# Half-size reloads of the second weight in a 20-product MLP behind sigmoid attention: single blocks kept in float32 and split on arrival, a new product order, a last store in three

## Chip, core and metric

The kernel runs on one core of one Trainium2 chip. The metric is the device time of one execution in microseconds. The engines are called as the profile calls them: PE (TensorE, matmul; PEld is its weight load), ACT (ScalarE), DVE (VectorE), POOL (GpSimd) and SP (SyncE, which here issues every DMA).

## What is computed

Eight batches of twelve heads, 448 tokens, head width 64. Attention uses a sigmoid instead of a softmax; its result, 3584 tokens by 768, goes through an MLP of width 2048.

```python
scores = scale * np.matmul(q, k.transpose(0, 1, 3, 2)) - np.log(S)
attn = 1.0 / (1.0 + np.exp(-scores))
attn_out = np.matmul(attn, v)
x = attn_out.transpose(0, 2, 1, 3).reshape(B * S, H * D)
h = x @ w_in
g = h * (1.0 / (1.0 + np.exp(-1.702 * h)))
return g @ w_out
```

All arrays are float32. The weights reach the kernel as raw words of a 64-bit type and are turned into float32 on the chip.

## The kernel before

**Precision.** Every float32 operand of a large product is held as two float32r parts: a rounded part `hi` and the rest `lo = value - hi`. A product of two such operands is three matmuls (lo by hi, hi by lo, hi by hi; `TERMS`, line 41). To "split" is to make the two parts: one copy that rounds (ACT or DVE, lines 759 and 760 for weights, 1001 and 1002 for activations) and one subtraction on DVE (lines 762 and 1013).

**Three stages.** Attention comes first; while it runs on PE, DVE and ACT decode the sixteen weight tiles (`decode`, line 456) and DMAs store twelve of them as float32 in DRAM (`whole`, names `f` in the trace). The tokens make seven blocks of 512. The first block is multiplied in the ordinary way (`first_block`, line 808): `up(n)` is a part of the first product (matmuls `h<-x,w`), `down(n)` a part of the second (matmuls `o_q<-g,w`), each `down` 36 matmuls long, in the order up 0, up 1, down 0, up 2, down 1, ..., up 7, down 6, down 7. Blocks 1 to 3 and 4 to 6 are two groups (`triple`, line 947). In a group each of the two weight products is replaced by 20 products of sums of blocks instead of 24 products of blocks (tables at lines 44 to 48): `W_SUMS`, `X_SUMS` and `G_SUMS` say which sums of weight and activation blocks enter product r, `H_SUMS` and `O_SUMS` how the 20 results are added. Each product is 36 matmuls of 128x512 (name `p`). `m` is 0 for the first weight and 1 for the second, `h` (0 or 1) is a half of a weight block.

**Weights in DRAM.** While the first block runs, the split parts of all twenty weight operands of both weights are saved in DRAM (`save`, line 772; DRAM names `c`), to be loaded by both groups. An operand is either a single block (six of the twenty: `W_USES[r] < 8`) or a sum of blocks. Single blocks are split for the first block's own use in `pieces` (line 814) and saved from there, two parts at once, 768 KB for each half: 12 saves for each weight (`c<-w` of 768 KB). Sums are made by `sums_ahead` (line 905) and saved (`c<-wc`); the right half of `h = 1` is made inside the first group from quarter loads (`wq<-f`).

**Weights in a group.** `pieces_of(m, r)` (line 965) takes a buffer from a ring of four (`wsplit`) for each half `h`, and loads the two parts from `c` (`w<-c`). A product uses two buffers, so the buffers of product k come free when product k-2 is done with them.

**Order of the work.** `SEQUENCES` (line 49) gives the order of the 40 products (m, r) of each group. It sets which x blocks (`x<-xd`, 768 KB each) are needed when, and how the results are added: `Net` decides by the distance between products whether a result goes on in PSUM (a chain), is put back there by ACT (a seed, line 1102), is copied out (line 1141) or is added by DVE out of PSUM (line 1175). Two PSUM tiles of four banks alternate.

**The planner.** The program's order on ACT, DVE and SP is made by `Plan.run` (line 104): a list scheduler with assumed costs. A task's `key` is the place of its first user in PE's order; an engine takes the ready task of least key. A task that needs a slot of SBUF may take one when its key is at most `HORIZON` = 14 tasks ahead. A DMA is assumed to end after all planned DMAs before it (2.7 ns for each KB) plus a landing time. The chip then runs each queue in that fixed order. `store` (line 1189) copies an output from PSUM where needed and issues its store; the last output of the second group is copied by ACT with a factor of -1 (line 1197), 1536 columns at once, then stored as 768 KB.

Of the kernel before, what the change touches and what calls it, by code (L numbers as in the profile page):

```python
# [8 lines left out]
F32 = mybir.dt.float32  # L9
# [23 lines left out]
HORIZON, URGENT, SPARE, KEEP = 14, 4, 1, 2  # L33
AWAY = 3

ATTENTION, LATE = ("qk", "vraw", "a", "al", "raw64", "e", "qkraw", "x32"), ("wsplit",)
# [11 lines left out]
O_SUMS = ([(20, [(9, 1), (17, -1)]), (21, [(5, 1), (10, 1)]), (22, [(4, 1), (12, 1)]), (23, [(21, 1), (22, -1)]), (24, [(18, 1), (23, 1)]), (25, [(1, 1), (11, 1)]), (26, [(0, 1), (20, 1)]), (27, [(25, 1), (26, 1)]), (28, [(8, 1), (15, 1)]), (29, [(3, 1), (13, 1)])], [[(4, -1), (6, -1), (20, 1), (28, 1)], [(9, 1), (19, 1), (24, 1)], [(1, -1), (7, 1), (24, 1), (29, 1)], [(12, -1), (16, 1), (27, -1), (28, -1)], [(5, -1), (14, -1), (27, -1)], [(0, -1), (2, 1), (21, -1), (29, -1)]])  # L48
SEQUENCES = ([(0, 16), (0, 18), (0, 19), (0, 12), (0, 3), (0, 10), (0, 8), (0, 14), (0, 11), (0, 2), (0, 5), (0, 15), (0, 17), (1, 3), (0, 1), (0, 4), (0, 7), (0, 13), (0, 6), (1, 8), (1, 4), (1, 18), (1, 12), (0, 9), (1, 5), (1, 16), (0, 0), (1, 19), (1, 2), (1, 13), (1, 15), (1, 9), (1, 10), (1, 14), (1, 7), (1, 1), (1, 0), (1, 6), (1, 17), (1, 11)], [(0, 18), (0, 19), (0, 14), (0, 10), (0, 3), (0, 12), (0, 13), (0, 2), (0, 1), (0, 5), (0, 11), (0, 17), (0, 7), (0, 9), (0, 15), (0, 0), (0, 6), (1, 2), (1, 9), (1, 0), (0, 16), (1, 3), (0, 4), (1, 5), (0, 8), (1, 10), (1, 16), (1, 4), (1, 15), (1, 8), (1, 13), (1, 19), (1, 17), (1, 12), (1, 1), (1, 6), (1, 18), (1, 14), (1, 11), (1, 7)])

# [27 lines left out]
class Plan:  # L78
# [25 lines left out]
    def run(self, streams):  # L104
# [43 lines left out]
        def since(t):  # L148
            when = t.ready
            for b in t.holds:  # L150
                if b.slot is None:
                    if not (t.anytime or t.key <= doing + HORIZON):
                        return math.inf
                    found = place(b, t)
                    if found is None:
                        return math.inf
                    when = max(when, found[0])
            return when
# [162 lines left out]
def sigmoid_attention_mlp(ctx: ExitStack, tc: tile.TileContext, qk, v, w, out):  # L321
# [486 lines left out]
    def first_block():  # L808
# [5 lines left out]
        def pieces(m, h, i, got):  # L814
            out = []
            for k in range(2):
                node = nodes[m, h, 2 * i + k] = got[k]
                b, into, first = (weights_slot if count[0] < 2 else weights_ring)(f"w{m}_{h}_{i}_{k}")
                t = split_piece(node, PIECE, into, b, first)
                if count[0] < 2:  # L820
                    for u in b.users:
                        u.anytime = True
                count[0] += 1
                for r in used_as(2 * i + k):
                    save(m, r, h, slice(0, PIECE), into, b, t)
                out.append((t, b, into))
            return out
# [119 lines left out]
    def triple(one, blocks_before):  # L947
# [17 lines left out]
        def pieces_of(m, r):  # L965
            out = []
            for h in range(2):
                b, into, first = weights_ring(f"w{m}_{one}_{r}_{h}")
                ts = []
                if W_USES[r] >= 8 and h and one == 1:  # L970
                    node = w_sums[m].get(W_USES[r])
# [52 lines left out]
        def products(m, r, sums, uses, n, parts, sign, onto, deps):  # L1024
            pieces = pieces_of(m, r)
            t_x, xb = pair_of(sums, uses[r][0], n, f"{'xg'[m]}p{one}_{uses[r][0]}", sign)
            ps, tag, more = onto
            edge = [*(blocks_before[tag] if len(plan.rings[tag]) == 1 else []), *deps]
            for i in range(parts):
# [14 lines left out]
                units_of.setdefault((m, r), []).append([t])  # L1044
            return t

        class Net:
# [34 lines left out]
            def product(self, r, onto):  # L1082
# [26 lines left out]
                t = products(self.m, r, sums, uses, (XB, GB)[self.m], self.parts, sign, (ps, tag, more), deps)  # L1109
                node = Node(ps, lambda: ps.tile[:, : self.parts].rearrange("p a b -> p (a b)"), [t])  # L1110
                if more:
# [76 lines left out]

        def store(i, sign, node, kind):
            if kind == "psum":  # L1190
                bank = node
                b, view = nets[1].slot(("out", i))
                if sign > 0:
                    t = on_either((act(XB), lambda: nc.scalar.copy(view(), bank.view())),
                                  (dve(XB), lambda: nc.vector.tensor_copy(view(), bank.view())), node.done, [b, node.b])
                else:
                    t = task("ACT", act(XB), lambda: nc.scalar.mul(view(), bank.view(), -1.0), node.done, [b, node.b])
                node.readers.append(t)
                node = Node(b, view, [t])
            else:  # L1200
                assert sign > 0
            k, n = divmod(i, 3)
            dma(lambda: out[one + n, k * NJ : (k + 1) * NJ].rearrange("j p t -> p j t"),
                lambda: node.view().rearrange("p (j t) -> p j t", j=NJ), P * XB * 4 / 1024, node.done, [node.b])

# [67 lines left out]
```

## Time and profile before

| | us |
|---|---|
| median of 3 runs | 1074.75 (1072.87 to 1075.59) |
| the profiled execution | 1073.19 |
| its span, first to last instruction | 1071.4 |
| PE busy in it | 1046.7 |
| DVE busy in it | 808.7 |
| ACT busy in it | 556.5 |
| mean granted TensorE clock (1 is 2.4 GHz) | 0.993 |

The span is what the trace covers; the profiled execution took 1.8 us more than that. PE is the bounding engine over most of the span, so idle time of the others matters only where PE waits for it. Attention takes about 0 to 263 us, the first block 263 to 402, the first group 408 to 735, the second 735 to 1065.

### The profile page before, as it was taken

The page shows a single profiled execution, that of the slowest core. Times are in us where ns is not written, and L with a number is a line of the kernel's source. Part 1 is how long each engine was busy: PE and PEld are TensorE (multiplying, and loading weights), DVE is VectorE, ACT ScalarE, POOL GpSimd, SP SyncE. Part 2 cuts the span into 40 slices and gives each one's busy share as a digit, 9 for nine tenths or more (in the row PEclk, how much of TensorE's full clock was granted, in tenths as well). Part 3 has the DMA queues.
Part 4 walks back from the last instruction along what each step waited for, and adds up shares of the span by engine and source line. Part 5 has one row for each costly group of instructions (what it writes and reads, how often), then busy time and mean ns, then how long its engine had stood idle before and what let it go on. Part 6 is the DMA issues. An engine that isn't in the chain of part 4 may idle for free.

```text
span 1071.4 us, 13585 instructions
## 1 busy us (share of the span) xinstructions
PE 1046.7 (98%) x5300; PEld 780.1 (73%) x5300; DVE 808.7 (75%) x733; ACT 556.5 (52%) x534; POOL 0.2 (0%) x4
## 2 busy tenths in 40 slices
PE   8999999999999987999999999999999999999997
PEld 5454545454788865888888888888888888888886
DVE  5988788873988755689789778997684676777683
ACT  7887888886555433545463344433444253433342
POOL 0000000000000000000000000000000000000000
PEclk9999999999999998999999999999999999999999
DMA  9899999883999999666677767699865656565665
GB/s 348 305 329 383 338 343 325 312 293 119 376 408 372 395 393 359 234 216 230 211 233 225 236 227 237 227 311 369 277 220 194 205 177 206 175 204 182 217 230 201
DMA packets 110799, 290.30 MB, mean 271 GB/s; under 512 B 8720, under 2 KB 69264, under 8 KB 108688
## 3 DMA queue, kind: packets, MB, share of 16 engines
q1 hardware_dynamic: 110736, 289.44, 76.6%
q8 instruction: 42, 0.69, 0.2%
q14 instruction: 21, 0.17, 0.0%
HBM read 195.04 MB, written 94.37 MB: 270 GB/s over the span
## 4 chain that ended last, share of the span: by engine, by line
PE 91%; DMA 6%; DVE 1%; ACT 1%; issue 1%; SPq 0%; DVEq 0%; ACTq 0%
PE p L796 60%; PE av L604 10%; PE sc L573 8%; PE h L796 5%; PE o_q L796 4%; DMA c<-wc 2%; PE av L617 2%; DMA x<-xd 1%; PE sc L589 1%; DMA xd<-x 1%; DMA wq<-f 1%; DMA qkraw<-qk 0%; DMA w<-c 0%; DVE qk L444 0%; ACT graw L852 0%
## 5 line engine op out<-in xcount | busy, mean ns | idle before, releaser
L796 PE MATMUL p<-xp,w 128*128 128x512 f32 x1440 | 330.5, 391 | 7.7 <-DVE xp L1013 5.9
L796 PE MATMUL p<-gp,w 128*128 128x512 f32 x1440 | 328.0, 389 | 0.1
L796 PEld LDWEIGHTS p<-xp,w 128*128 128x128 f32 x1440 | 271.6, 189 | 65.4 <-DVE xp L1013 6.3
L796 PEld LDWEIGHTS p<-gp,w 128*128 128x128 f32 x1440 | 270.2, 188 | 56.6 <-DMA w<-c 0.5
L559 ACT ACTIVATE a<-sc,bias 128x896 f32<-128x896 f32 x168 | 158.5, 1019 | 15.1 <-PE sc L573 10.9
L604 PE MATMUL av<-a,vraw 128*64 128x448 f32 x576 | 118.6, 547 | 0.1
L573 PEld LDWEIGHTS sc<-qk 64*128 64x128 f32 x846 | 75.8, 184 | 41.9 <-issue 13.8
L573 PE MATMUL sc<-qk 64*128 64x448 f32 x846 | 98.6, 373 | 3.4 <-DVE qk L444 2.3
L604 PEld LDWEIGHTS av<-a,vraw 128*64 128x64 f32 x576 | 37.1, 136 | 59.7 <-issue 56.1
L1141 ACT COPY o<-p 128x1536 f32<-128x1536 f32 x23 | 33.1, 1445 | 90.3 <-PE p L796 60.9
L1141 ACT COPY h<-p 128x2048 f32<-128x2048 f32 x19 | 35.6, 1874 | 78.1 <-PE p L796 59.6
L796 PE MATMUL o_q<-g,w 128*128 128x512 f32 x288 | 68.5, 396 | 5.2 <-ACT w L759 3.5
L1013 DVE TENSOR_TENSOR gp<-h,gp 128x2048 fp32r<-128x2048 f32 x29 | 66.4, 2289 | 5.7 <-ACT gp L1001 5.3
L1175 DVE TENSOR_TENSOR h<-h,p 128x2048 f32<-128x2048 f32 x20 | 45.3, 2286 | 31.9 <-ACT h L1141 17.8
L796 PEld LDWEIGHTS o_q<-g,w 128*128 128x128 f32 x288 | 54.9, 192 | 17.9 <-ACT w L759 3.9
L796 PE MATMUL h<-x,w 128*128 128x512 f32 x288 | 66.6, 390 | 1.3 <-DVE x L656 1.3
L796 PEld LDWEIGHTS h<-x,w 128*128 128x128 f32 x288 | 54.0, 188 | 13.3 <-DVE x L656 2.1
L444 DVE TENSOR_TENSOR qk<-qkraw,qk 128x896 fp32r<-128x896 f32 x47 | 51.2, 1089 | 6.1 <-ACT qk L438 5.6
L1001 ACT CAST gp<-h 128x2048 fp32r<-128x2048 f32 x19 | 36.3, 1913 | 36.9 <-PE p L796 28.6
L1175 DVE TENSOR_TENSOR o<-o,p 128x1536 f32<-128x1536 f32 x20 | 34.7, 1751 | 23.0 <-PE p L796 13.9
L739 DVE TENSOR_TENSOR h<-h,h 128x2048 f32<-128x2048 f32 x21 | 48.0, 2289 | 0.5 <-ACT h L1183 0.2
L656 DVE COPY x<-av 128x64 f32<-128x64 f32 (+6 forms) x42 | 16.9, 413 | 36.0 <-ACT x L654 31.2
(106 smaller groups left out, 963.2 us busy)
## 6 DMA issues: line engine op xcount, KB each, us to landing
w<-c SPq DMA_DIRECT2D x76, 768.0 KB, 5.2
w<-c SPq DMA_DIRECT2D x140, 384.0 KB, 4.4
w<-w SPq DMA_DIRECT2D x16, 1536.0 KB, 10.2
c<-wc SPq DMA_DIRECT2D x56, 384.0 KB, 7.4
qkraw<-qk SPq DMA_DIRECT2D x47, 448.0 KB, 6.4
c<-w SPq DMA_DIRECT2D x24, 768.0 KB, 7.6
vraw<-v SPq DMA_DIRECT2D x24, 448.0 KB, 4.9
xd<-x SPq DMA_DIRECT2D x42, 256.0 KB, 4.7
```

The source lines that it names most:

```text
L444: lambda: nc.vector.tensor_tensor(lo(), src(), hi().bitcast(F32), op=ALU.subtract),
L559: nc.scalar.activation(a.tile, ps.tile[:, :, :S], AF.Sigmoid, bias=bias, scale=scale)
L573: nc.tensor.matmul(ps.tile[:, j, :S], lhsT=src[kk][rows, S + c * P : S + (c + 1) * P], rhs=src[qq][rows, :S], start=i == 0, stop=i == len( ...
L604: nc.tensor.matmul(ps.tile[cols, n % 2, :S], lhsT=vr.tile[:, at : at + D], rhs=a.tile[:, j], start=c == 0, stop=False, skip_group_check=True,)
L617: nc.tensor.matmul(ps.tile[cols, k, :S], lhsT=vr.tile[rows, at : at + D], rhs=a.tile[rows, j], start=False, stop=True, skip_group_check=True,)
L656: (0.15 + 0.00105 * n, lambda xb=xb, into=into, cols=cols: nc.vector.tensor_copy(xb.tile[:, into], ps.tile[:, bank, cols])),
L739: return task("DVE", cost, lambda: nc.vector.tensor_tensor(out(), x(), y(), op=op), deps, uses)
L796: nc.tensor.matmul(ps, lhsT=ws[:, a, c * P : (c + 1) * P], rhs=x[:, d, k], start=start and i == 0 and j == 0, stop=stop and i == len(todo) ...
L1001: t_hi = on_either((act(n), lambda: nc.scalar.copy(part(0)(), node.view())), (cast(n), lambda: nc.vector.tensor_copy(part(0)(), node.view())),
L1013: nc.vector.tensor_tensor(part(1)(), node.view(), part(0)().bitcast(F32), op=ALU.subtract)
L1141: t = on_either((act(self.n), lambda: nc.scalar.copy(view(), node.view())), (dve(self.n), lambda: nc.vector.tensor_copy(view(), node.view())),
L1175: nc.vector.tensor_tensor(view(), x.view(), y.view(), op=ALU.add if s0 == s else ALU.subtract)
```

## The change

**Reloads.** For the second weight (`AGAIN`: m = 1, both halves) the saves of split single blocks in `pieces` are left out: 12 saves of 768 KB. In both groups `pieces_of` loads such a block (six products for each group, two halves each, 24 loads) in float32 from `whole`, 384 KB, into the second part of its ring buffer, and splits it there: the rounding copy on ACT or DVE, the subtraction on DVE.

**Planner.** A DMA whose key lies more than `PRESSING` = 4 tasks ahead isn't planned to start before the planned DMA backlog is down to `BACKLOG` = 6 us.

**Order.** The first group has a new sequence; that of the second stays.

**Last store.** Where the last output of the second group comes out of PSUM, its three 512-column parts are copied and stored one by one, each after the matmuls of that part. `products` therefore returns the task of each part.

```diff
+AGAIN = ((1, 0), (1, 1))
+BACKLOG, PRESSING = 6.0, 4
...
-SEQUENCES = ([(0, 16), (0, 18), (0, 19), (0, 12), (0, 3), (0, 10), (0, 8), (0, 14), (0, 11), (0, 2), (0, 5), (0, 15), (0, 17), (1, 3), (0, 1), (0, 4), (0, 7), (0, 13), (0, 6), (1, 8), (1, 4), (1, 18), (1, 12), (0, 9), (1, 5), (1, 16), (0, 0), (1, 19), (1, 2), (1, 13), (1, 15), (1, 9), (1, 10), (1, 14), (1, 7), (1, 1), (1, 0), (1, 6), (1, 17), (1, 11)], [...
+SEQUENCES = ([(0, 19), (0, 8), (0, 10), (0, 18), (0, 2), (0, 16), (0, 12), (0, 1), (0, 14), (0, 15), (0, 11), (0, 7), (0, 17), (0, 4), (0, 0), (0, 5), (1, 8), (0, 9), (0, 3), (1, 4), (1, 12), (0, 13), (1, 3), (1, 18), (0, 6), (1, 16), (1, 9), (1, 10), (1, 2), (1, 19), (1, 14), (1, 15), (1, 17), (1, 7), (1, 1), (1, 13), (1, 11), (1, 0), (1, 5), (1, 6)], [...
...
         def since(t):
             when = t.ready
+            if "SP" in t.costs and t.key > doing + PRESSING:
+                when = max(when, free["DMA"] - BACKLOG)
...
-                for r in used_as(2 * i + k):
+                for r in used_as(2 * i + k) if (m, h) not in AGAIN else ():
                     save(m, r, h, slice(0, PIECE), into, b, t)
...
                 b, into, first = weights_ring(f"w{m}_{one}_{r}_{h}")
                 ts = []
+                if W_USES[r] < 8 and (m, h) in AGAIN:
+                    i, k = divmod(W_USES[r], 2)
+                    n = (2 * m + h) * 4 + i
+                    at = k * NW_EL
+                    t = dma(lambda into=into: into()[:, 1].bitcast(F32), lambda n=n, at=at: whole[n][:, at : at + NW_EL],
+                            KB, [stored[n], *gate], [b], first)
+                    t = split_piece(Node(b, lambda into=into: into()[:, 1].bitcast(F32), [t]), PIECE, into, b)
+                    out.append(([t], b, into))
+                    continue
...
+                last = one + 3 == NB and all(left < 0 for left in nets[1].left.values())
+                parts = [slice(j, j + 1) for j in range(NJ)] if last else parts
...
+            for end, part in zip(ends, parts):
+                cols = slice(part.start * T, part.stop * T)
...
+                    else:
+                        end = task("ACT", act(n), lambda cols=cols, copied=copied: copied(nc.scalar.mul, cols, -1.0),
+                                   [end], [b, bank.b])
+                    bank.readers.append(end)
+                done.append(end)
+                dma(lambda part=part: into[:, part], lambda cols=cols: view()[:, cols].rearrange("p (j t) -> p j t", t=T),
+                    P * n * 4 / 1024, [end], [b])
```

## Rows read from the trace of the kernel before

**Rows 1.** The page: busy time of each engine; DMA busy in 40 slices.
```profile
PE 1046.7 (98%) x5300; PEld 780.1 (73%) x5300; DVE 808.7 (75%) x733; ACT 556.5 (52%) x534; POOL 0.2 (0%) x4
...
DMA  9899999883999999666677767699865656565665
```

**Rows 2.** Timeline of PE, 350 to 425 us: start, us, work, idle before and its releaser.
```profile
379.21 8.32 PE L796 MATMUL o_q<-g,w 128*128 128x512 f32 x36
391.06 0.49 PE L796 MATMUL o_q<-g,w 128*128 128x512 f32 x1 [3.53 <-ACT w L759]
392.05 9.62 PE L796 MATMUL o_q<-g,w 128*128 128x512 f32 x35 [0.50 <-DVE w L762]
407.56 10.60 PE L796 MATMUL p<-xp,w 128*128 128x512 f32 x36 [5.89 <-DVE xp L1013]
419.94 5.25 PE L796 MATMUL p<-xp,w 128*128 128x512 f32 x22 [1.78 <-issue]
```

**Rows 3.** Timeline of ACT from 1060 us to the end.
```profile
1065.53 1.45 ACT L1197 ACTIVATE o<-p 128x1536 f32<-128x1536 f32 x1 [13.39 <-PE p L796]
```

**Rows 4.** Windows of 20 us: each engine's busy time, then PEclk, DMA share, GB/s.
```profile
280.00:300.00 20.00, 18.89 (x83) 15.67 (x84) 19.90 (x31) 11.19 (x16) 0.00 (x0) 1.00 1.02 377
...
320.00:340.00 20.00, 20.00 (x90) 16.57 (x89) 17.04 (x29) 11.27 (x19) 0.00 (x0) 1.00 0.98 360
...
380.00:400.00 20.00, 15.98 (x64) 12.58 (x63) 10.89 (x19) 7.67 (x13) 0.00 (x0) 0.91 1.03 387
400.00:420.00 20.00, 12.33 (x45) 9.37 (x43) 6.82 (x7) 6.72 (x6) 0.00 (x0) 0.83 1.04 413
```

**Rows 5.** What PE waited for from 0 to 366 us: total, times, longest.
```profile
PE sc L573 <- DVE qk L444: 2.3, 2, 1.8
```

**Rows 6.** The chain that ended last, between 340 and 425 us: start, us, what.
```profile
379.68 6.78 DMA wq<-f
...
394.15 10.06 DMA x<-xd
404.24 1.48 ACT xp L1001
```

**Rows 7.** A window of 2.5 us, columns as in rows 4.
```profile
422.50:425.00 2.50, 2.50 (x12) 2.07 (x12) 2.50 (x3) 0.00 (x0) 0.00 (x0) 1.00 0.33 127
```

**Rows 8.** DMAs issued from 366 to 425 us; the last column is the median us to landing.
```profile
DMA packets 9080, 22.80 MB, mean 386 GB/s; under 512 B 684, under 2 KB 6253, under 8 KB 9077
...
x<-xd SPq DMA_DIRECT2D x4, 768.0 KB, 10.2
c<-w SPq DMA_DIRECT2D x3, 768.0 KB, 8.5
```

**Rows 9.** DMAs issued from 750 to 1060 us, columns as in rows 8.
```profile
w<-c SPq DMA_DIRECT2D x82, 384.0 KB, 4.3
w<-c SPq DMA_DIRECT2D x33, 768.0 KB, 4.4
```

**Rows 10.** Groups by line and shape: count | busy us, mean ns | idle before, releasers.
```profile
L1013 DVE TENSOR_TENSOR gp<-h,gp 128x2048 fp32r<-128x2048 f32 x29 | 66.4, 2289 | 5.7 <-ACT gp L1001 5.3
L1175 DVE TENSOR_TENSOR o<-o,p 128x1536 f32<-128x1536 f32 x20 | 34.7, 1751 | 23.0 <-PE p L796 13.9 <-ACT o L1141 9.0
L762 DVE TENSOR_TENSOR w<-wf,w 128x768 fp32r<-128x768 f32 x16 | 15.0, 956 | 5.0 <-ACT w L759 4.9
L759 ACT CAST w<-wf 128x768 fp32r<-128x768 f32 x13 | 10.8, 839 | 23.1 <-PE o_q L796 13.4 <-DMA wf<-f 9.7
L897 ACT COPY o<-o_q 128x512 f32<-128x512 f32 x2 | 1.2, 588 | 2.3 <-PE o_q L796 1.7 <-DMA c<-wc 0.6
```

**Rows 11.** Timeline of SP's DMA issues near the end of the second group.
```profile
1039.63 2.53 SPq L412 DMA_DIRECT2D w<-c  x4
```

**Rows 12.** Five products long, the end of the first group; columns as in rows 4.
```profile
693.10:733.90 40.80, 40.80 (x182) 33.78 (x181) 38.99 (x28) 15.17 (x11) 0.00 (x0) 1.00 0.94 332
```

**Rows 13.** DMAs issued from 1060 us to the end, columns as in rows 8.
```profile
out<-o SPq DMA_DIRECT2D x3, 768.0 KB, 3.6
```

More of the change, by code (lines that the diff above doesn't have):

```diff
@@ L48 @@
 O_SUMS = ([(20, [(9, 1), (17, -1)]), (21, [(5, 1), (10, 1)]), (22, [(4, 1), (12, 1)]), (23, [(21, 1), (22, -1)]), (24, [(18, 1), (23, 1)]), (25, [(1, 1), (11, 1)]), (26, [(0, 1), (20, 1)]), (27, [(25, 1), (26, 1)]), (28, [(8, 1), (15, 1)]), (29, [(3, 1), (13, 1)])], [[(4, -1), (6, -1), (20, 1), (28, 1)], [(9, 1), (19, 1), (24, 1)], [(1, -1), (7, 1), (24, 1), (29, 1)], [(12, -1), (16, 1), (27, -1), (28, -1)], [(5, -1), (14, -1), (27, -1)], [(0, -1), (2, 1), (21, -1), (29, -1)]])
-SEQUENCES = ([(0, 16), (0, 18), (0, 19), (0, 12), (0, 3), (0, 10), (0, 8), (0, 14), (0, 11), (0, 2), (0, 5), (0, 15), (0, 17), (1, 3), (0, 1), (0, 4), (0, 7), (0, 13), (0, 6), (1, 8), (1, 4), (1, 18), (1, 12), (0, 9), (1, 5), (1, 16), (0, 0), (1, 19), (1, 2), (1, 13), (1, 15), (1, 9), (1, 10), (1, 14), (1, 7), (1, 1), (1, 0), (1, 6), (1, 17), (1, 11)], [(0, 18), (0, 19), (0, 14), (0, 10), (0, 3), (0, 12), (0, 13), (0, 2), (0, 1), (0, 5), (0, 11), (0, 17), (0, 7), (0, 9), (0, 15), (0, 0), (0, 6), (1, 2), (1, 9), (1, 0), (0, 16), (1, 3), (0, 4), (1, 5), (0, 8), (1, 10), (1, 16), (1, 4), (1, 15), (1, 8), (1, 13), (1, 19), (1, 17), (1, 12), (1, 1), (1, 6), (1, 18), (1, 14), (1, 11), (1, 7)])
+SEQUENCES = ([(0, 19), (0, 8), (0, 10), (0, 18), (0, 2), (0, 16), (0, 12), (0, 1), (0, 14), (0, 15), (0, 11), (0, 7), (0, 17), (0, 4), (0, 0), (0, 5), (1, 8), (0, 9), (0, 3), (1, 4), (1, 12), (0, 13), (1, 3), (1, 18), (0, 6), (1, 16), (1, 9), (1, 10), (1, 2), (1, 19), (1, 14), (1, 15), (1, 17), (1, 7), (1, 1), (1, 13), (1, 11), (1, 0), (1, 5), (1, 6)], [(0, 18), (0, 19), (0, 14), (0, 10), (0, 3), (0, 12), (0, 13), (0, 2), (0, 1), (0, 5), (0, 11), (0, 17), (0, 7), (0, 9), (0, 15), (0, 0), (0, 6), (1, 2), (1, 9), (1, 0), (0, 16), (1, 3), (0, 4), (1, 5), (0, 8), (1, 10), (1, 16), (1, 4), (1, 15), (1, 8), (1, 13), (1, 19), (1, 17), (1, 12), (1, 1), (1, 6), (1, 18), (1, 14), (1, 11), (1, 7)])
 def act(n):
@@ L1026, in products @@
             t_x, xb = pair_of(sums, uses[r][0], n, f"{'xg'[m]}p{one}_{uses[r][0]}", sign)
-            ps, tag, more = onto
+            (ps, tag, more), done = onto, []
             edge = [*(blocks_before[tag] if len(plan.rings[tag]) == 1 else []), *deps]
@@ L1044, in products @@
                 units_of.setdefault((m, r), []).append([t])
-            return t
+                done.append(t)
+            return done
         class Net:
@@ L1109, in product @@
                 t = products(self.m, r, sums, uses, (XB, GB)[self.m], self.parts, sign, (ps, tag, more), deps)
-                node = Node(ps, lambda: ps.tile[:, : self.parts].rearrange("p a b -> p (a b)"), [t])
+                node = Node(ps, lambda: ps.tile[:, : self.parts].rearrange("p a b -> p (a b)"), t[-1:])
+                node.each = t
                 if more:
@@ L1189, in store @@
         def store(i, sign, node, kind):
+            k, n = divmod(i, 3)
+            into, bank = out[one + n, k * NJ : (k + 1) * NJ].rearrange("j p t -> p j t"), node
+            parts = [slice(0, NJ)]
             if kind == "psum":
-                bank = node
+                last = one + 3 == NB and all(left < 0 for left in nets[1].left.values())
+                parts = [slice(j, j + 1) for j in range(NJ)] if last else parts
                 b, view = nets[1].slot(("out", i))
[L1193 to L1197, printed above, removed]
@@ L1198, in store @@
-                node.readers.append(t)
-                node = Node(b, view, [t])
+                node, ends = Node(b, view, []), node.each if last else node.done
             else:
                 assert sign > 0
-            k, n = divmod(i, 3)
-            dma(lambda: out[one + n, k * NJ : (k + 1) * NJ].rearrange("j p t -> p j t"),
-                lambda: node.view().rearrange("p (j t) -> p j t", j=NJ), P * XB * 4 / 1024, node.done, [node.b])
+                b, view, ends = node.b, node.view, node.done
@@ new lines, in store, with copied @@
+            done = []
+            for end, part in zip(ends, parts):
+                cols = slice(part.start * T, part.stop * T)
+                n = cols.stop - cols.start
+                if kind == "psum":
+                    def copied(op, cols=cols, *more):
+                        return op(view()[:, cols], bank.view()[:, cols], *more)
+                    if sign > 0:
+                        end = on_either((act(n), lambda cols=cols, copied=copied: copied(nc.scalar.copy, cols)),
+                                        (dve(n), lambda cols=cols, copied=copied: copied(nc.vector.tensor_copy, cols)),
+                                        [end], [b, bank.b])
+                    else:
+                        end = task("ACT", act(n), lambda cols=cols, copied=copied: copied(nc.scalar.mul, cols, -1.0),
+                                   [end], [b, bank.b])
+                    bank.readers.append(end)
+                done.append(end)
+                dma(lambda part=part: into[:, part], lambda cols=cols: view()[:, cols].rearrange("p (j t) -> p j t", t=T),
+                    P * n * 4 / 1024, [end], [b])
```

## Prediction, made before the changed kernel was run

> **What bounds the kernel now.** I read the page first. PE is busy for 98% of the span [rows 1], so the only things worth having are the places where PE waits or runs slowly, and a change in the other engines' work counts only through those. The second line of those rows shows the DMA engines full in slices 11 to 16 (about 270 to 430 us) and at five to seven tenths in most later ones: look for a DMA-bound stretch around the change of stage. The timeline of PE finds it. Down 7 ought to start one product after down 6 did. The second product of the first group starts at 419.94 and the last matmul of all ends when ACT takes its result at 1065.53 [rows 2, 3]; between these lie 79 products, so one takes 645.6 / 79 = 8.17 us with no stop of weight. From 379.21 the next starts should be 387.4 (down 7), 395.6 (first product p) and 403.7 (second p). The second p started at 419.94 [rows 2]: **16.2 us are lost in this one place**, 11.7 as four waits (3.53, 0.50, 5.89, 1.78) and the rest because the clock was granted at half (1.2 instead of 2.4 GHz) for part of it, so that 35 matmuls took 9.62 and 36 took 10.60 [rows 2], with means of 0.91 and 0.83 in the two windows [rows 4]. Of all the rest, attention's waits for a split are the largest, 2.3 us [rows 5].
>
> What ends these waits last? In the chain [rows 6] it is DMA: a quarter load of a weight that took 6.78 us, and the x block for the first p, issued at 394.15 and landed 10.06 later; from there 3.35 us of splitting lead to the start of p at 407.56 [rows 2]. In the seven windows from 280 to 420 us the DMA share is 0.98 to 1.04, lowest at 320 [rows 4], and it falls to 0.33 at 422.5 [rows 7]. DMAs issued between 366 and 425 us took 10.2 us to land for a 768 KB x block [rows 8], where 4.4 us is usual for 768 KB when the queue is half empty [rows 9]: about 6 us of queue stood ahead of each. So the stretch is bound by bytes, at 386 GB/s [rows 8].
>
> **The change, part by part.** The sum is made against the profiled execution, 1073.19 us (span 1071.4 and 1.8 around it); that is 1.6 under the median of the runs.
>
> *Saves left out.* 12 saves of 768 KB (786,432 bytes) are 9.44 MB, at 386 GB/s 24.4 us of the full queue. They are issued by the eight downs between 281 and about 407 us. If the queue would otherwise stay full, all but the last move the x block's landing forward: 11 x 2.04 = 22 us. If the time freed before 366 us is only idled away, because the next saves wait for DVE anyway, what counts is the 3 saves issued after 366 us [rows 8], 6.1 us, and perhaps the 6 us of queue standing at 366. So the relief lies between 6 and 22 us, with 12 for the case that also loses the standing queue. Needed: 12 us for the first p (its x at 392 instead of 404.2), and for the second p more: its inputs must be split by 403.7. I take a value near the upper half, since the share never fell under 0.98 between 280 and 420 [rows 4].
>
> *New order, at its start.* The first product now uses weight block 0 as it is; the old one used a sum whose right half came from four quarter loads and three sums, and such a load stands in the chain with 6.78 us [rows 6]. That goes. Against it, the first three products need x blocks 1, then 0 and 3, then 5 and 2: five loads of 768 KB where the old order needed three (3, then 1 and 2). Two more loads are 1.57 MB, 4.1 us of queue at the same rate, due by the third p.
>
> *Planner rule.* It holds back saves, so that loads needed soon stand behind about 6 us of planned queue at most instead of all of it. On SP this moves saves behind x and weight loads; what waits for a save is its slot. The trace of before can't show it. Its bounds are the largest thing of the kind seen elsewhere, 2.3 us either way [rows 5]; I take 0.
>
> Together for the stretch: 16.2 can be won at most; I leave 2.5 of it (the second and third p with their extra x loads) and take **-13.7**. Bounds -16.2 and -2 (6.1 of relief less 4.1 for the two loads).
>
> *Reload and split.* 24 loads of 384 KB instead of 768 KB take another 9.44 MB away, in the groups, where PE isn't waiting for DMA: nothing gained. Added are 24 rounding copies (0.84 us on ACT) and 24 subtractions of 0.956 us on DVE [rows 10], 23 us in all over 650 us. They lie under PE as long as a product's two halves are ready when it starts. The lead is known from the row of four loads issued at 1039.63 [rows 11] for a product that starts two products before 1065.53, at 1049.2: 9.6 us (the first half of a block is done with a little before the product ends; the second is needed as much later). Needed: 4.3 us to land [rows 9] + 0.84 + 2 x 0.956 (the two subtractions in a row) = 7.05. What is left, 2.5 us, covers one DVE operation of 2.29 us in the way [rows 10], not two. Bounds: 0, and 12 products x 2.1 us (two in the way: 7.05 + 4.58 - 9.6 = 2.0, rounded up for handovers) = 25. The plan puts the split first by key, so I stay near the lower end: **+1**.
>
> The rows say that half the bytes land 0.1 us sooner (4.3 and 4.4 us [rows 9]). The Trainium skill speaks to this price, on its page DMA: Bandwidth & Descriptors, section Anatomy of one DMA: about 2.0 us of fixed cost and bytes at 436 GB/s (a fit of the other issuing path, GpSimd's). By that, as an estimate, 384 KB would land 0.9 us sooner than 768 KB, and the split would have 0.8 us more lead in each of the 12 products; the rows don't show this gain.
>
> *New order, its additions.* Counted from the tables with the rules of `Net`: old order 17 seeds, 33 copies, 32 additions; new order 12, 29 and 36. DVE gets 8.6 us more that only it can do (3 more of 2.29 and 1 more of 1.755 us [rows 10]), ACT or DVE loses 9 operations. The place that matters is the last five products of the first group, where DVE was already busy 38.99 of 40.8 us [rows 12]. There the new order has 14 additions x 1.751 = 24.5, five rests of g pairs and three sums of g, 8 x 2.289 = 18.3, four new subtractions = 3.8 and five half-width weight operations at 0.6, a little over half of the 0.956, = 3.0: 49.6 us for 40.8. But 8 of the 14 additions (14.0 us) read no PSUM and feed only stores of outputs; nothing on PE waits for them, and the second group's start has room. What must be done in time is 35.6. Bounds 0 and 8.8; I take **+0.5**.
>
> *Last store.* Now: 1.45 us of ACT after the last matmul [rows 3], then a 768 KB store, 3.6 us to landing [rows 13], of which 2.0 are its bytes at the rate above. New: the last 512 columns take 0.59 us on ACT [rows 10] and 256 KB need 0.7 + 1.6 = 2.3 us; the other two parts end under the last 5.4 us of matmuls. 0.86 + 1.3 = **-2.2**; bounds -2.2 and -0.9 (the store no shorter). By the page just named, as an estimate, the 256 KB store would take 2.6 us, and the part -1.9.
>
> Sum: 1073.19 - 13.7 + 1 + 0.5 - 2.2 = **1058.8 us**.
>
> **The rivals.**
> A. *The bytes freed early are idled away.* SP would find DVE's sums no sooner than now, so the queue runs empty before 366 us and only 6.1 us are won (the further x loads then stand ahead of saves and cost nothing). For it: DVE was full (19.90 of 20) at 280 us [rows 4]. Against it: the share stayed at 0.98 or more throughout [rows 4]. 1073.19 - 6.1 + 1 + 0.5 - 2.2 = 1066.4, with a spread of 1062 to 1071.
> B. *Slower: the split comes too late.* In each of the 12 products of single blocks PE waits at its start, because two DVE operations stand between landing and subtraction. 12 x 2.1 = 25 in place of 1: 1082.8. It makes the kernel slower from (13.7 + 2.2 + 3) / 12 = 1.6 us for each product on. For it: DVE is full at the end of the first group [rows 12], and the four buffers allow no earlier load. Against it: one operation in the way still fits, and the rounding copy can go to ACT, busy 15.17 of 40.8 us there [rows 12].
> C. *The change doesn't do what it says:* the stretch stays full, because the relief of 6.1 is eaten by the two further x loads (-2 is left), and the crowd of additions costs part of its 8.8 at the end of the group: 1073.19 - 2 + 1 + 3.5 - 2.2 = 1073.5.
>
> **How the numbers follow.** The forecast (1055 to 1062) gets 0.60, A 0.18, B 0.09, C 0.08, and 0.05 goes to better than 1055, which needs all of the 16.2 and no new wait (1073.19 - 16.2 - 2.2 = 1054.8). For 8 times in 10 the range takes in the forecast, the best case down to 1054 and A up to 1068; outside stay B, C and the poor end of A, about 0.2. A measurement of this kernel can tell 0.3%, 3.2 us, from no change: faster means under 1071.5. Forecast, best case and A lie there: 0.83; C is the same: 0.08; B is slower: 0.09.
>
> **What would show it.** Right: PE's timeline without a wait between 379 and 420 us and with a full clock there; x loads for the first p landing before about 392; the DMA share below 1 in most windows from 280 to 400; the first p starting near 396; after the last matmul 0.6 us of ACT and a store of 256 KB. Each of these is a term of the sum. Wrong: PE waiting for the rounding copy or subtraction of a w piece inside the groups (B); the DMA share falling before 366 while x still lands late (A); a wait for DVE near 700 to 740 us or an x load still queued past 400 (C). The prediction is wrong above all if the loads that PE waits for are held by slots or by SP's order instead of by bytes.

## The result and the profile after

| | us |
|---|---|
| before, median of 4 runs | 1074.24 |
| changed kernel, median of 4 runs (1060.78 to 1062.76) | 1061.38 |
| ratio | 0.9882 (95% interval 0.9865 to 0.9899) |
| profiled execution of the changed kernel, and its span | 1060.78, 1059.0 |
| forecast | 1058.8 (1054 to 1068) |

The kernel is 1.2% faster, as was forecast in direction and nearly in size. The sum behind it is another matter: its parts (change of stage, groups, last store) were off by 2.6 to 3.4 us each and partly cancelled, so that the sum came so near is in part luck.

The timeline of PE around the change of stage, changed kernel (columns as in rows 2; p is the name of the matmuls of a group's products), and windows as in rows 4:

```profile
378.38 16.48 PE L800 MATMUL o_q<-g,w 128*128 128x512 f32 x72
394.70 35.52 PE L800 MATMUL p<-xp,w 128*128 128x512 f32 x156
```
```profile
380.00:400.00 20.00, 20.00 (x90) 16.58 (x89) 14.36 (x15) 4.76 (x5) 0.00 (x0) 1.00 1.02 398
400.00:420.00 20.00, 20.00 (x90) 16.57 (x89) 12.30 (x12) 6.69 (x7) 0.00 (x0) 1.00 0.80 265
```

Where [rows 2] had four waits, there is none, and the clock is granted in full (1.00 for the 0.91 and 0.83 of [rows 4]). The first p starts at 394.70, so the second, one product of 8.16 us later, at 402.86 instead of 419.94: **17.1 us won** (0.8 of them ahead of this stretch, since down 6 starts at 378.38 instead of 379.21). But the DMA share between 380 and 400 is still 1.02. The queue stayed full; what left it is what PE was waiting behind. A block of x issued between 366 and 425 us now lands in 8.4 us instead of 10.2, a 768 KB weight load in 5.3 instead of 8.9:

```profile
DMA packets 7642, 18.98 MB, mean 322 GB/s; under 512 B 590, under 2 KB 5197, under 8 KB 7639
...
w<-c SPq DMA_DIRECT2D x6, 768.0 KB, 5.3
x<-xd SPq DMA_DIRECT2D x5, 768.0 KB, 8.4
```

Most of the gain is an earlier issue. SP issued the first x load at 394.15 before [rows 6] and issues it at 373.88 now; ACT began to split that block at 404.24 before and begins at 381.89 now. Of these 22.4 us, 20.3 are the earlier issue and 2.1 the shorter way to landing (SP's and ACT's timelines, changed kernel):

```profile
373.88 2.21 SPq L416 DMA_DIRECT2D x<-xd  x3
...
381.89 1.49 ACT L1014 CAST xp<-x 128x1536 fp32r<-128x1536 f32 x1 [1.20 <-DMA x<-xd]
```

What was given back lies inside the groups and at the end. The rows of PE's timeline with an idle time, 575 us to the end (the first two stand in the 24th product):

```profile
583.51 1.66 PE L800 MATMUL p<-gp,w 128*128 128x512 f32 x6 [0.97 <-DVE gp L1026]
585.98 7.14 PE L800 MATMUL p<-gp,w 128*128 128x512 f32 x30 [0.81 <-DMA w<-c]
...
625.96 54.37 PE L800 MATMUL p<-gp,w 128*128 128x512 f32 x237 [0.21 <-DVE gp L1026]
...
905.06 8.50 PE L800 MATMUL p<-xp,w 128*128 128x512 f32 x36 [0.99 <-DVE xp L1026]
...
1050.59 3.01 PE L800 MATMUL p<-gp,w 128*128 128x512 f32 x12 [0.75 <-ACT o L1222]
```

Before the change PE had no wait of this size after 420 us. The last of these rows is the new store: PE's last 12 matmuls wait for ACT, which is copying another part of the same result. The end of ACT's timeline shows the other side of it (to be set beside [rows 3]):

```profile
1049.94 0.60 ACT L1222 ACTIVATE o<-p 128x512 f32<-128x512 f32 x1 [10.67 <-PE p L800]
1053.64 1.09 ACT L1222 ACTIVATE o<-p 128x512 f32<-128x512 f32 x2 [3.10 <-PE p L800]
```

The first part was complete after a third of the product's 8.2 us, some 5.4 us before the product's end, yet ACT took it at 1049.94, when the second part was done; the second and third both went after the last matmul.

### The profile page after: what moved, and what is told of

Read it like the earlier page. It is cut to its first block, busy times and chain, and to the rows that moved or that the text cites. A ratio compares the mean times of both kernels' runs of the same rounds, so it can differ in the third digit from the quotient of the medians.

```text
span 1059.0 us, 13676 instructions
## 1 busy us (share of the span) xinstructions
PE 1043.6 (99%) x5300; PEld 777.5 (73%) x5300; DVE 843.4 (80%) x770; ACT 554.5 (52%) x543; POOL 0.2 (0%) x4
## 4 chain that ended last, share of the span: by engine, by line
PE 89%; DVE 4%; DMA 3%; ACT 2%; issue 1%; SPq 0%; ACTq 0%; DVEq 0%
PE p L800 54%; PE av L608 11%; PE sc L577 9%; PE h L800 6%; PE o_q L800 6%; PE av L621 2%; PE sc L593 2%; DMA qkraw<-qk 1%; DMA w<-c 1%; DMA w<-f 1%; DMA c<-wc 1%; DVE gp L1026 1%; ACT gp L1014 1%; DVE h L743 0%; ACT o L1156 0%
## 5 line engine op out<-in xcount | busy, mean ns | idle before, releaser
L1026 DVE TENSOR_TENSOR gp<-h,gp 128x2048 fp32r<-128x2048 f32 x31 | 70.9, 2288 | 9.3 <-ACT gp L1014 8.9
L1190 DVE TENSOR_TENSOR h<-h,p 128x2048 f32<-128x2048 f32 x23 | 52.1, 2284 | 18.6 <-PE p L800 11.4
L1014 ACT CAST gp<-h 128x2048 fp32r<-128x2048 f32 x23 | 44.0, 1912 | 43.5 <-PE p L800 36.2
L1156 ACT COPY o<-p 128x1536 f32<-128x1536 f32 x18 | 25.9, 1443 | 59.3 <-PE p L800 19.2
L743 DVE TENSOR_TENSOR h<-h,h 128x2048 f32<-128x2048 f32 x24 | 54.7, 2285 | 0.1
L763 ACT CAST wc<-ws 128x384 fp32r<-128x384 f32 (+1 forms) x57 | 32.2, 580 | 42.2 <-DVE ws L743 26.8
L1014 ACT CAST xp<-x 128x1536 fp32r<-128x1536 f32 x19 | 28.1, 1480 | 39.4 <-PE p L800 32.3
```

Of the source, the lines that this page charges most:

```text
L743: return task("DVE", cost, lambda: nc.vector.tensor_tensor(out(), x(), y(), op=op), deps, uses)
L763: t_hi = on_either((act(n), lambda: nc.scalar.copy(into()[:, 0], node.view())), (cast(n), lambda: nc.vector.tensor_copy(into()[:, 0], node ...
L1014: t_hi = on_either((act(n), lambda: nc.scalar.copy(part(0)(), node.view())), (cast(n), lambda: nc.vector.tensor_copy(part(0)(), node.view())),
L1026: nc.vector.tensor_tensor(part(1)(), node.view(), part(0)().bitcast(F32), op=ALU.subtract)
L1156: t = on_either((act(self.n), lambda: nc.scalar.copy(view(), node.view())), (dve(self.n), lambda: nc.vector.tensor_copy(view(), node.view())),
L1190: nc.vector.tensor_tensor(view(), x.view(), y.view(), op=ALU.add if s0 == s else ALU.subtract)
```

## The experiments

All ratios are against the kernel before on the same chip. The chips differ: the kernel before has medians of 1073.69 to 1074.75 us on them, so small differences between rows are better read from the ratios.

| run | order | saves left out | split on arrival | planner rule | last store | median us | ratio (95%) |
|---|---|---|---|---|---|---|---|
| changed kernel | new | 12 | 24 | 6 us | in three | 1061.38 | 0.988 (0.987 to 0.990) |
| reload alone | old | 12 | 24 | no | whole | 1077.10 | 1.002 (1.001 to 1.004) |
| order alone | new | 0 | 0 | no | whole | 1084.88 | 1.011 (1.008 to 1.013) |
| rule alone | old | 0 | 0 | 8 us | whole | 1061.32 | 0.988 (0.985 to 0.991) |
| without the rule | new | 12 | 24 | no | in three | 1061.56 | 0.988 (0.987 to 0.989) |
| saves issued again | new | 0 | 24 | no | in three | 1084.62 | 1.010 (1.007 to 1.013) |
| old order | old | 12 | 24 | 6 us | in three | 1074.94 | 1.001 (0.999 to 1.002) |
| half the reload | new | 6 | 12 | 6 us | three copies after | 1062.98 | 0.989 (0.986 to 0.992) |
| half, old order | old | 6 | 12 | 6 us | three copies after | 1079.27 | 1.004 (1.002 to 1.006) |
| no split | new | 12 | 0 | 6 us | in three | 1060.97 | 0.988 (0.986 to 0.989) |
| no split, old order | old | 12 | 0 | no | whole | 1058.60 | 0.986 (0.983 to 0.988) |
| store whole | new | 12 | 24 | 6 us | whole | 1060.54 | 0.987 (0.985 to 0.989) |
| copies after | new | 12 | 24 | 6 us | three copies after | 1060.10 | 0.987 (0.985 to 0.989) |

### What closed the stretch: bytes, order or priority

**Reload alone**, on the kernel before:

```diff
+AGAIN = ((1, 0), (1, 1))
-                for r in used_as(2 * i + k):
+                for r in used_as(2 * i + k) if (m, h) not in AGAIN else ():
...
+                if W_USES[r] < 8 and (m, h) in AGAIN:
```

> The kernel before with one part of the change: the 12 saves of the second weight's single blocks are left out, and the groups reload these blocks in float32 and split them. Old order, no planner rule, last store whole. Bytes theory (the stretch of 16.2 us around the change of stage is bound by DMA bytes, and 9.44 MB less frees it): it closes by 11 to 16 us, first p at 395 to 400 us, time 1058 to 1064. Priority theory (what matters is that loads needed soon stand behind saves): most of the wait stays, since nothing is put ahead, time 1068 or more. Order theory (the old first product's quarter loads and sums are what is late): time 1066 or more.

**Order alone**, on the kernel before, is the one line `SEQUENCES`.

> The kernel before with the new order of the first group alone; all saves stay, loads of split parts as before. Order theory: first p by 400 us, time 1060 to 1066. Bytes theory: the queue stays full, and two more x loads are due by the third p, so little or nothing is won: 1070 to 1078. The stretch of DVE around the 23rd product, where the changed kernel waits 1.8 us, belongs to the order by either theory, and should show here too.

**Rule alone**, on the kernel before:

```diff
+BACKLOG, PRESSING = 8.0, 4
...
+            if "SP" in t.costs and t.key > doing + PRESSING:
+                when = max(when, free["DMA"] - BACKLOG)
```

> The kernel before with the planner rule alone, with a backlog of 8 us instead of 6 us; old order, all saves. Priority theory: loads that PE waits for pass the saves, first p by 400 us, time 1060 to 1065. Bytes theory: the saves put off keep their slots and have to go through the same queue before the groups start, so at most some 4 us are won: 1070 to 1075.

**Without the rule**: the changed kernel less these two lines.

> The changed kernel without the planner rule. Bytes theory: the stretch stays closed, first p at 395 to 397 us, time 1059 to 1063; if the late weight load before the 24th product of the first group comes from saves that the rule pushed in front of it, that wait of 0.8 us is gone and the time is some 1 us less. Priority theory: the waits of the stretch come back by 6 us or more, time 1067 or more.

**Saves issued again**: the run without the rule, with

```diff
-                for r in used_as(2 * i + k) if (m, h) not in AGAIN else ():
+                for r in used_as(2 * i + k):
```

> The changed kernel without the planner rule, as the run before without it, but the 12 saves of the second weight's single blocks are issued again; nothing reads them. New order, reloads and the last store in three stay. Bytes theory: 9.44 MB more in a full queue bring the waits around the change of stage back, first p at 405 us or later, time 1072 to 1085. Rival (the new order or the reloads closed the stretch, not the bytes): first p at 396 to 399, time 1060 to 1063.

With the rule kept, the saves can't be issued again: the planner comes to a point at which no task can begin, so this combination has no time.

The first rows of p in PE's timeline between 375 and 430 us, in this order: reload alone, order alone, rule alone, saves issued again (without the rule there is no wait either, first p at 395.93). In the order alone and with the saves issued again, down 6 waits 2.92 and 0.49 us besides, for a rounding copy and a subtraction:

```profile
396.12 34.16 PE L797 MATMUL p<-xp,w 128*128 128x512 f32 x150
```
```profile
409.38 10.69 PE L796 MATMUL p<-xp,w 128*128 128x512 f32 x36 [8.49 <-DVE xp L1013]
425.03 5.22 PE L796 MATMUL p<-xp,w 128*128 128x512 f32 x16 [4.95 <-issue]
```
```profile
397.32 26.41 PE L799 MATMUL p<-xp,w 128*128 128x512 f32 x108 [2.04 <-DMA w<-c]
424.09 6.18 PE L799 MATMUL p<-xp,w 128*128 128x512 f32 x26 [0.36 <-DVE xs L742]
```
```profile
408.58 10.95 PE L798 MATMUL p<-xp,w 128*128 128x512 f32 x36 [10.09 <-DVE xp L1024]
424.48 124.10 PE L798 MATMUL p<-xp,w 128*128 128x512 f32 x540 [4.95 <-issue]
```

In either order the saves decide: without them no wait (reload alone; without the rule), with them the waits stand (the kernel before; saves issued again). So the saves, 9.44 MB, are the cause in both orders. But they need not go: the rule alone keeps them all and leaves 2.4 us of the waits. It moved saves to where PE needs nothing: 10 saves of sums (`c<-wc`, 384 KB) are issued between 395 and 440 us where it were 4, and the share from 420 to 440 us is 0.97 instead of 0.62.

SP's timelines show by what. With all saves and no rule SP issues the first x load at 393.40 to 394.62 us (the kernel before, order alone, saves issued again); in the other three runs of this section it does so at 375.37 to 378.82. With the rule alone the block takes 9.7 us from issue to the start of its split, against 10.1 before: the queue is as full as it was, and the whole gain is the place in SP's order. What costs is the bytes that SP has put ahead of the awaited load. Whether these bytes hold it by their time in the queue alone, or also by slots that come free only when a save has landed, these runs don't separate: in the chain of the kernel before, the x load is issued at 394.15, 0.06 us after this save has landed.

```profile
386.61 7.48 DMA c<-wc
```

Of the theories, bytes foresaw the closed stretch of the reload alone (first p at 396.12), but not its time (1077.10 for 1058 to 1064, because of waits inside the groups) and not the rule alone (1061.32 for 1070 to 1075). Priority foresaw the rule alone, but not the closed stretch of the reload alone. They are no rivals: the loads were late because saves stood before them, and one may drop the saves or put them behind. The order theory is wrong: the new order alone is 1.1% slower, which is beyond what any theory expected; its second p starts 5 us later than before. The wait around the 24th product that was expected here too isn't there; one of 2.83 us for a weight load stands in the 32nd.

### What was given back inside the groups

Reload alone closes the stretch and is still slower than before. Its profiled execution took 1079.94 us, the longest of its ten, so the waits shown are on the high side. Its rows of PE's timeline with the longest waits, and the chain that ended last between 622 and 642 us:

```profile
582.00 8.72 PE L797 MATMUL p<-gp,w 128*128 128x512 f32 x30 [3.27 <-DMA w<-c]
638.59 75.25 PE L797 MATMUL p<-gp,w 128*128 128x512 f32 x318 [5.71 <-DMA w<-c]
...
719.09 24.87 PE L797 MATMUL p<-gp,w 128*128 128x512 f32 x102 [2.58 <-DMA w<-c]
```
```profile
627.80 0.55 DVE w L763
628.36 2.20 DVE gp L1023
630.56 0.48 DVE ws L740
...
631.06 0.37 DVE wc L761
...
631.46 0.57 DVE wc L763
...
632.04 2.76 DMA c<-wc
...
634.88 3.67 DMA w<-c
...
638.59 3.78 PE p L797 x8
```

PE stops after the sixth matmul of a product, where it comes to the second half (`h = 1`) of its weight. The operand is a sum of blocks, not a reloaded one. The chain runs: DVE comes late to the sum (`ws`) and to its split (`wc`); the two parts are saved (2.76 us), and SP, which takes its queue in order, waits for the save to land before it issues the load of the same data (3.67 us). The save and the load alone take 6.4 us of a product's 8.2. In the changed kernel the wait of 0.81 us is of this kind: SP stood 6.6 us for the landing of a save of a sum, ahead of weight loads.

```profile
SPq L416 <- DMA c<-wc: 7.6, 2, 6.6
SPq L416 <- DVE ws L743: 3.8, 1, 3.8
```

Two edits take the split away and leave the saves out as they are; one on the changed kernel, one on the reload alone. Both load blocks of the first weight in place of the second's, so their results are not those of the task; only their times count:

```diff
-                    t = dma(lambda into=into: into()[:, 1].bitcast(F32), lambda n=n, at=at: whole[n][:, at : at + NW_EL], ...
-                    t = split_piece(Node(b, lambda into=into: into()[:, 1].bitcast(F32), [t]), PIECE, into, b)
+                    t = dma(lambda into=into: into().bitcast(F32), in_dram(0, r, h, WHOLE), 2 * KB, ...
```

> The changed kernel with the reload's split left out: the products of single blocks of the second weight load, from DRAM, the two split parts of the first weight's block (768 KB, as before the change), so these products compute with other weights. No save comes back. Split theory (the 24 subtractions and their rounding copies crowd DVE, sums come late, and loads wait for their saves): the waits inside the groups, 3.1 us, shrink below 1, time 1058 to 1059. Order theory (the additions and sums of the new order crowd DVE by themselves): the waits stay at 2 to 3 us, time 1060.5 to 1061.5.

> The run with the reload alone (old order, no planner rule), but the split left out: the products of single blocks of the second weight load the two split parts of the first weight's block (768 KB), so they compute with other weights; the 12 saves stay left out. Crowd theory (the reload's rounding copies and 24 subtractions put DVE behind, and sums of the second weight are saved late and loaded back late): the 14.6 us of waits inside the groups fall below 4, time 1058 to 1062. Rival (leaving the saves out alone reorders what is made ahead, and the late sums come from that): the waits stay at 8 us or more, time 1068 to 1077.

In the old order this settles it: 1058.6 instead of 1077.1, although each of these loads is twice as large again. PE's busy time from 560 to 740 us, reload alone and then without the split:

```profile
560.00:740.00 180.00, 166.48 (x704) 135.27 (x704) 147.83 (x128) 70.58 (x59) 0.00 (x0) 0.96 0.64 210
```
```profile
560.00:740.00 180.00, 180.00 (x795) 148.81 (x794) 152.17 (x119) 72.54 (x57) 0.00 (x0) 1.00 0.79 267
```

So the splits cost 18.5 us there. Of the 14.6 us of waits in the groups 11.6 are for loads of sums as above and 2 for the rests of activations on DVE. None is put down to a split piece itself; 0.8 us have no releaser in the profile. DVE is not full over the whole stretch (147.8 of 180); the splits put sums off in its order. Whether that comes of DVE's time in those products or only of the other order that the planner makes with them, these runs don't separate.

In the new order the picture is mixed. Without the split the waits of 0.97, 0.81, 0.21 and 0.99 us are gone, but another of the same kind stands in the 32nd product:

```profile
652.10 73.97 PE L800 MATMUL p<-gp,w 128*128 128x512 f32 x318 [2.78 <-DMA w<-c]
```

A wait of 2.7 to 2.8 us in that place is also in the order alone and in half the reload, so it comes with the new order; the full set of splits shifts it away and puts 3 us elsewhere. The split theory's 1058 to 1059 failed; the order theory's values came out (waits of 2 to 3 us, and 1060.97 for 1060.5 to 1061.5), with the wait in another product. In the new order, then, the splits have no price that shows: 1061.38 with them, 1060.97 without.

**Old order** (the changed kernel with the old `SEQUENCES`), **half the reload** (`AGAIN = ((1, 0),)`, last output as in the run of copies after) and the two together:

> The changed kernel with the old order of the first group: reload, planner rule and last store in three stay. Crowd theory (with the reload's subtractions in the old order DVE falls behind, sums are saved late, and loads stand behind these saves on SP): waits of 8 to 15 us inside the first group as in the run with the reload alone, time 1070 to 1078. Rival (the rule, which lets needed loads pass, cures these waits too): 4 us of waits or less, time 1058 to 1063.

> The changed kernel with the reload for half h = 0 of the second weight alone (6 saves left out instead of 12, 12 reloads and splits instead of 24), the three copies of the last output after the last matmul as in the run with that edit. Bytes theory: 4.7 MB less is 12 us of queue, about the 16 us needed together with the rule, so the first p starts at 395 to 399. Crowd theory: with half the subtractions the waits inside the groups shrink to 2 us or less. Time 1057 to 1061; 1062 or more if the stretch needs all 12 saves gone.

> As the run with half the reload, but with the old order of the first group. Bytes theory for the stretch: first p at 395 to 399. Crowd theory inside the group: half the subtractions, and no more additions than before, so between the 0.5 us of waits of the rule alone and the 14 of the reload alone: 1058 to 1066.

Old order: 1074.94, the stretch closed and 10.4 us of waits for weight loads in the group, at the same products as in the reload alone. The new order is what makes the splits bearable: with it 1061.4, without it 1074.9. Half the reload: the stretch closes but for 0.70 us, but waits of 2.73 and 0.94 us stand in the group where 2 or less were expected, and the time, 1062.98, is above its expectation. Half in the old order fell outside its expectation altogether: besides 5.73 us for a load of a sum in the group, two waits come back at the change of stage, the longer one before the second p:

```profile
397.61 8.44 PE L800 MATMUL p<-xp,w 128*128 128x512 f32 x36 [1.27 <-issue]
415.13 99.85 PE L800 MATMUL p<-xp,w 128*128 128x512 f32 x432 [9.07 <-issue]
```

DVE's sum of two x blocks for that p began at 409.97, released, by the profile, by the landing of a save, and SP had waited 9.9 us for saves of sums between 380 and 416 us, while the DMA share from 400 to 420 us was 0.89:

```profile
409.97 1.76 DVE L743 TENSOR_TENSOR xs<-x,x 128x1536 f32<-128x1536 f32 x1 [1.13 <-DMA c<-wc]
```

DVE's own order stands in the way too: the operation that DVE took up before this sum, the rounding copy of another x block at 406.09, had itself waited 8.11 us for the first p. So there it isn't bytes alone that hold the p, but slots and the fixed orders of SP and DVE, which wait for saves to land and for PE. Which of these is worth how much is open.

### The store in three

**Store whole** sets `last = False`. **Copies after** lets each of the three copies depend on the whole product and lets DVE take one:

```diff
-                node, ends = Node(b, view, []), node.each if last else node.done
+                node, ends = Node(b, view, []), node.done * len(parts)
```

> The changed kernel, only the last output copied and stored whole as before. Theory of a false order: the copy of one part and the matmuls of the next wait for each other, since they touch one tile, so in the changed kernel PE loses about 1 us in the last product and the copies still end after it; whole, PE has no wait there, the span ends 5.9 us after the last matmul, and the time is 0 to 1 us less than the changed kernel's 1061.4. Rival (the store in three wins what was forecast): 1.5 to 2.2 us more, 1063 to 1063.6.

> The changed kernel, last output in three parts, but all three copies after the last matmul, on ACT or DVE, each with its store. Theory of a false order: no wait of PE in the last product, the copies end 1.1 to 1.2 us after the last matmul, the last 256 KB land some 4.4 to 5 us after it: 1059.4 to 1060.5. Rival (the order is no matter): as the changed kernel or some 0.5 us more, 1061 to 1062.

The ends of ACT's and DVE's timelines, store whole, then copies after:

```profile
1053.65 1.45 ACT L1222 ACTIVATE o<-p 128x1536 f32<-128x1536 f32 x1 [13.39 <-PE p L800]
```
```profile
1052.17 0.60 ACT L1222 ACTIVATE o<-p 128x512 f32<-128x512 f32 x1 [13.39 <-PE p L800]
...
1052.80 0.69 DVE L1230 TENSOR_SCALAR o<-p 128x512 f32<-128x512 f32 x1 [3.56 <-ACT o L1222]
1053.52 0.60 ACT L1222 ACTIVATE o<-p 128x512 f32<-128x512 f32 x1 [0.76 <-DVE o L1230]
```

In both, PE has no wait in the last product. From the last matmul to the end of the span it takes 1059.7 - 1053.65 = 6.05 us whole, 1057.1 - 1052.17 = 4.93 with the copies after, and 1059.0 - 1053.64 = 5.36 in the changed kernel, which pays 0.75 of PE's wait and a slow start of the last 12 matmuls on top. Counted so, the copies after lose least and the changed kernel most, and the medians (1060.10, 1060.54, 1061.38) lie in this order but within each other's spread, so the order rests on these rows. The false order is shown a second time: with the copies after, DVE waits for ACT and ACT for DVE, though each reads other columns of PSUM and writes other columns of the result; the copies end 1.95 us after the last matmul where 1.1 to 1.2 were expected. In this program the waits go by the tile, not by the columns. Copies after, at 1060.10, is the fastest of these kernels that compute with the right weights; it is no more than 1.3 us better than the changed one.

## Why the prediction was right, and which steps were wrong

Against the profiled executions, term by term:

| term | forecast | measured | from |
|---|---|---|---|
| change of stage | -13.7 | -17.1 | second p at 402.86 for 419.94 |
| splits and additions in the groups | +1.5 | +4.3 | last matmul 650.8 us after the second p, for 645.6; less 0.9 in the last product; 3.0 of the rest are the four waits above |
| last store | -2.2 | +0.4 | 5.36 after the last matmul for 5.87, and 0.9 lost before it (the last 540 matmuls take 123.9 us, with the store whole 123.0) |
| sum | -14.4 | -12.4 | 1060.78 for 1073.19 |

**Right: what the 16.2 us are.** The reading of the four waits, the half clock and the chain as one loss that goes back to the saves held: the run with the saves issued again brings it back, the reload alone takes it away. The relief was at the upper end: the first x block is split 22.4 us sooner, where the prediction's case of a queue that stays full gives 22. So rival A, in which the freed time is idled away, is out. The 2.5 us left over for the further x loads were not needed.

**In part wrong: how the saves hold the loads.** The prediction takes "about 6 us of queue" ahead of each load, from 10.2 us for an x block against 4.4 for a weight load. The x blocks issued from 750 to 1060 us took 6.5 us, so the like comparison gives 3.7. And the queue's length is the smaller part: 2.1 of the 22.4 us. Its last sentence sets bytes against SP's order; the runs show that both act, as the bytes that stand ahead in SP's order.

**Wrong: a sign named for it.** The DMA share was to fall below 1 in most windows between 280 and 400; it is 0.99 to 1.03 there. Later transfers moved up into the room (42 saves of sums issued by 395 us, 39 before; five x loads, one before). A full queue does no harm by itself; what stands before the awaited load does.

**Right as a term, wrong in its reason: the planner rule.** It was set at 0 with bounds of 2.3 us, taken from attention's waits, a place that has nothing to do with it. On top of the reload it does add nothing (1061.38 with, 1061.56 without), but that is luck of the company: alone, with 8 us, it wins 12.4 us. The step that failed is the choice of the row: the rows that bear on it were those of the full stretch itself [rows 8], where a rule can put the saves behind the loads.

**Wrong: the order taken as a gain at its start.** Dropping the quarter loads ahead of the first p was counted for it; alone the order costs 1.1%. The price set against it, 4.1 us for two further x loads, is near what the order alone shows (second p 5.1 us later). Its worth lies where the prediction saw only a risk, inside the first group, and only together with the splits: 13.6 us between the old and the new order. Why this order bears the splits is not shown.

**Mis-sized: the splits.** Rival B came nearest to the size in the old order (25 us; the splits cost 18.5 there, 14.6 in waits and more at half clock behind them) and the condition (DVE operations in the way), and the wrong place: the prediction priced the piece that is split, whose lead indeed suffices, and not the work that the split pushes back. What is late is a sum that DVE makes for another operand, and SP's queue then adds a save and a load to it. The lead of 9.6 us per piece was the wrong test; the right one would have followed the least urgent work on DVE to its own deadline. That the forecast still held is due to the new order.

The price of the half-size load was read from another kind of load. Over the whole changed kernel the reloads (`w<-f`) landed in 3.5 us, other loads of 384 KB (`w<-c`) in 4.4:

```profile
w<-c SPq DMA_DIRECT2D x140, 384.0 KB, 4.4
w<-c SPq DMA_DIRECT2D x52, 768.0 KB, 4.6
...
w<-f SPq DMA_DIRECT2D x24, 384.0 KB, 3.5
```

So a piece had 0.8 us more lead than the 4.3 us of the sum left it, one more reason why no split piece was late. The estimate that the prediction makes by the Trainium skill (DMA: Bandwidth & Descriptors, Anatomy of one DMA), 0.9 us between 384 and 768 KB, is near what the reloads show (1.1 us) and not what `w<-c` shows (0.2 us). Why the two kinds differ is not shown.

**Wrong: the last store.** It was taken for granted that copies by part follow matmuls by part. The step that failed is "the other two parts end under the last 5.4 us of matmuls". Nothing in the trace of before showed a copy out of a tile that PE was still writing, and the term got no bound above zero for that; it needed one. The three stores of 256 KB took 3.2 us to land, too, where the sum has 2.3.

## What to carry to other kernels

When loads wait in a full DMA queue, ask first what stands ahead of them: leaving traffic out and putting it behind are both cures, and the second may cost nothing. Work that is added to an engine with time to spare is paid by its least urgent task; follow that task to its deadline, above all where its result goes through DRAM and back on an in-order queue. Splitting a result into parts helps only if the program's waits know parts: look whether they go by the tile.

## What the runs showed of the hardware that was not expected

A save of 384 KB to DRAM and the load of the same data behind it took 2.76 + 3.67 us from issue to landing in the reload alone, at a DMA share of 0.17 to 0.37 between 632 and 636 us. That is three quarters of a product (8.2 us), and some 2 us of it are bytes at the rate of [rows 8].

The granted clock of TensorE stayed at 1.00 (2.4 GHz) behind the single waits of about 1 us in the changed kernel, from 580 to 590 and from 900 to 910 us. Behind the waits of 3.27 and 5.71 us in the reload alone it fell to the lower level (1.2 GHz): means of 0.57 from 582 to 584 and 0.50 from 638 to 642 us, and 30 matmuls took 8.72 us behind the first where the changed kernel's took 7.14.
